# Sixty-four leftover rows of a contraction as row-tile pairs, and two weights side by side as one 512-column operand

## The chip, the cores and the metric

One core of one Trainium2 chip. The metric is the time of one execution in device microseconds, as the median of several runs.

## The reference

The model mixes two branches of an input x of 2048 x 576 with a learned gate, and returns the output and the gradients of everything:

```python
g   = sigmoid((x * gate_w).sum(-1))
a   = irfft2(rfft2(x) * (w_r + 1j * w_i))                 # global filter, 2-D FFT
b   = (gelu(x @ w_gate) * (x @ w_up)) @ w_down            # D=576 -> F=4608 -> D
out = g * a + (1 - g) * b
# and the vjp of out with grad_out: A_x, w_r, w_i, w_gate, w_up, w_down, gate_w
```

All in bf16. D = 576 = 4 x 128 + 64. Every product that contracts over D has four full chunks of 128 rows and one tail of 64.

## The kernel before

The loop that the change touches has 18 groups of 256 columns of F, with 8 steps each: 144 steps. A step takes 256 of the 2048 rows (two tiles of 128) and makes three products that contract over D: gate and up (x with w_gate, w_up) and dA (grad_out with w_down transposed). ScalarE takes them out of PSUM (the accumulator memory; the comments say how the pools divide its banks):

```python
ph = ps1.enter_context(tc.tile_pool(name="ph", bufs=4, space=PSUM))   # 1 bank each: products
pw = ps1.enter_context(tc.tile_pool(name="pw", bufs=2, space=PSUM))   # 1 bank each: weight gradients
pf = ps1.enter_context(tc.tile_pool(name="pf", bufs=1, space=PSUM))   # 2 banks, one buffer: FFT units

nc.gpsimd.memset(xT[0:D4NEW, 4, :, :], 0.0)      # 64 zero rows: the tail is padded to 128
...
def H_mm(g, tp):
    wg_g, wu_g, wdT_g = wts[g]
    out = []
    for w, xt in ((wg_g, xT), (wu_g, xT), (wdT_g, dOT)):
        pt = ph.tile([P, TPB, FG], F32, tag="hps", name="hps")         # FG = 256, TPB = 2
        for tt in range(TPB):
            for ci in range(5):
                nc.tensor.matmul(pt[:, tt, :], lhsT=xt[:, ci, tp * TPB + tt, :], rhs=w[:, ci, :],
                                 start=(ci == 0), stop=(ci == 4))
        out.append(pt)
    return out

def H_ew1(g, tp, pts):                            # VectorE's part of the chain cut
    hg, hu_ps, da_ps = pts
    ...
    nc.scalar.activation(q[:], hg[:], ACT.Square)
    nc.scalar.copy(xb[:], hg[:])
    ...
    nc.scalar.copy(hu[:], hu_ps[:])
    nc.scalar.activation(om[:], s[:], ACT.Sigmoid, scale=-2.0 * C_GELU)
    nc.scalar.activation(s[:], s[:], ACT.Sigmoid, scale=2.0 * C_GELU)
    ...                                           # for the two row tiles:
        nc.scalar.activation(da[:, tt, :], da_ps[:, tt, :], ACT.Copy, scale=omg32[:, t0 + tt:t0 + tt + 1])
```

The gap between the products of two steps is filled with FFT units (all through the one buffer `pf`) and with weight-gradient units of the group before:

```python
quota = [0, 1, 1, 1, 2, 1, 2, 1]                  # weight-gradient units by step of the group
for g in range(NG):
    for tp in range(NT):
        step = g * NT + tp
        fft_until(want(step, 0))                  # FFT unit(s) ahead of the products
        pts = H_mm(g, tp)
        tiles = H_ew1(g, tp, pts)                 # ScalarE: q, xb, hu, om, s, da
        fft_until(want(step, 1))                  # FFT unit(s) behind them
        H_ew2(g, tp, tiles)
        ...
        for _ in range(quota[tp]):
            if pend:
                pend.pop(0)()                     # weight-gradient units
```

Each FFT unit is some matmuls into `pf` and one copy out of it (its drain), mostly on ScalarE, so the drain stands in ScalarE's program behind the `da` of its step.

## Time and profile before

| | before |
|---|---|
| median of 4 runs (range) | 1579.05 us (1577.83 to 1579.81) |
| span of the profiled run | 1576.6 us |
| start: up to q of step 8 | 84.7 us |
| loop: q of step 8 to q of step 143 | 1016.2 us |
| rest | 475.7 us |

I cut the span at ScalarE's q of step 8 and of step 143. The table by stretches for these three parts of the kernel before: length, then busy time and instructions of TensorE, its weight loads, VectorE, ScalarE and GpSimd, then granted clock (the share of full speed that TensorE was given by the clock record), DMA share and GB/s.

```profile
0.00:84.70 84.70, 55.82 (x508) 44.98 (x509) 55.52 (x160) 58.33 (x101) 8.49 (x25) 0.90 0.64 165
84.70:1101.00 1016.30, 994.94 (x9043) 859.09 (x9041) 673.98 (x1816) 653.82 (x1251) 0.00 (x0) 1.00 0.42 117
1101.00:1576.60 475.60, 459.33 (x3764) 366.84 (x3761) 84.43 (x178) 26.63 (x45) 17.84 (x33) 0.99 0.85 171
```

TensorE works for 994.9 of the loop's 1016 us.

### The profile page before, as it was taken

The page shows a single profiled execution, that of the slowest core. Times are in us where ns is not written, and L with a number is a line of the kernel's source. Part 1 is how long each engine was busy: PE and PEld are TensorE (multiplying, and loading weights), DVE is VectorE, ACT ScalarE, POOL GpSimd, SP SyncE. Part 2 cuts the span into 40 slices and gives each one's busy share as a digit, 9 for nine tenths or more (in the row PEclk, how much of TensorE's full clock was granted, in tenths as well). Part 3 has the DMA queues.
Part 4 walks back from the last instruction along what each step waited for, and adds up shares of the span by engine and source line. Part 5 has one row for each costly group of instructions (what it writes and reads, how often), then busy time and mean ns, then how long its engine had stood idle before and what let it go on. Part 6 is the DMA issues. An engine that isn't in the chain of part 4 may idle for free.

```text
span 1576.6 us, 33157 instructions
## 1 busy us (share of the span) xinstructions
PE 1510.1 (96%) x13310; PEld 1270.9 (81%) x13310; DVE 813.9 (52%) x2154; ACT 738.8 (47%) x1395; POOL 26.3 (2%) x58
## 2 busy tenths in 40 slices
PE   6798999999999999999999999999997999999998
PEld 4577888888788888888888888888876777777776
DVE  5775565666887877865555646667103212121210
ACT  6777665765766766665666656656000000000000
POOL 1000000000000000000000000000000000000000
PEclk8999999999999999999999999999999999999999
DMA  6632432334544544453424434364899978787873
GB/s 140 198 102 78 113 99 82 109 97 132 140 134 120 151 124 129 132 152 93 124 82 135 127 97 128 101 145 122 241 192 214 212 153 172 155 171 154 170 150 69
DMA packets 513435, 214.45 MB, mean 136 GB/s; under 512 B 318080, under 2 KB 506368, under 8 KB 513280
## 3 DMA queue, kind: packets, MB, share of 16 engines
q1 hardware_dynamic: 511648, 207.61, 54.5%
q0 software_dynamic: 1632, 4.72, 1.1%
q8 instruction: 104, 1.70, 0.5%
q14 instruction: 51, 0.42, 0.1%
HBM read 41.77 MB, written 94.71 MB: 87 GB/s over the span
## 4 chain that ended last, share of the span: by engine, by line
PE 62%; issue 23%; DVE 6%; ACT 6%; DMA 1%; POOL 1%; SPq 1%; POOLq 0%; DVEq 0%; ACTq 0%
PE hps L312 25%; PE wps L392 15%; PE wps L376 7%; PE pf L640 3%; PE acc L833 2%; PE wps L403 2%; PE pf L433 2%; PE acc L875 2%; ACT da L334 1%; ACT om L330 1%; ACT q L323 1%; DMA pin<-scr 1%; PE pf L624 1%; PE pf L626 1%; ACT xb L324 1%
## 5 line engine op out<-in xcount | busy, mean ns | idle before, releaser
L312 PEld LDWEIGHTS <-xT 128*128 128x128 bf16 x2880 | 286.0, 99 | 39.6
L875 PEld LDWEIGHTS <-pin 128*128 128x128 bf16 x2304 | 225.4, 98 | 58.3 <-DMA pin<-scr 1.6
L392 PEld LDWEIGHTS <-xn 128*128 128x128 bf16 x2304 | 223.9, 98 | 30.3 <-issue 3.6
L312 PE MATMUL hps<-wg_g,xT 128*128 128x256 bf16 x1440 | 186.5, 278 | 0.0
L312 PE MATMUL hps<-wu_g,xT 128*128 128x256 bf16 x1440 | 183.8, 275 | 0.0
L312 PE MATMUL hps<-wdT_g,dOT 128*128 128x256 bf16 x1440 | 180.8, 273 | 0.0
L325 DVE TENSOR_SCALAR s<-q 128x512 bf16<-128x512 bf16 x144 | 42.0, 291 | 254.0 <-ACT q L323 253.8
L312 PEld LDWEIGHTS <-dOT 128*128 128x128 bf16 x1440 | 141.0, 98 | 16.4
L833 PE MATMUL acc<-wd_all,pin 128*128 128x288 bf16 x1152 | 145.4, 288 | 8.1 <-DMA pin<-scr 6.6
L376 PE MATMUL wps<-dB,A 128*128 128x288 bf16 x1152 | 152.2, 286 | 0.0
L875 PE MATMUL acc<-wuT,pin 128*128 128x288 bf16 x1152 | 143.4, 286 | 1.3 <-DMA pin<-scr 1.3
L833 PEld LDWEIGHTS <-pin 128*128 128x128 bf16 x1152 | 113.2, 98 | 38.5 <-DMA pin<-scr 7.5
L875 PE MATMUL acc<-wgT,pin 128*128 128x288 bf16 x1152 | 143.4, 286 | 0.0
L376 PEld LDWEIGHTS <-A 128*128 128x128 bf16 x1152 | 112.7, 98 | 27.6
L392 PE MATMUL wps<-dHu,xn 128*128 128x256 bf16 x1152 | 131.7, 273 | 0.0
L392 PE MATMUL wps<-dHg,xn 128*128 128x256 bf16 x1152 | 131.5, 273 | 0.0
L323 ACT ACTIVATE q<-hps 128x512 bf16<-128x512 f32 x144 | 86.1, 598 | 94.9 <-PE hps L312 94.9
L885 ACT COPY f32t<-acc 128x576 f32<-128x576 f32 x16 | 10.2, 638 | 250.5 <-PE acc L875 250.5
L334 ACT ACTIVATE da<-hps,omg 128x256 bf16<-128x256 f32 x288 | 118.1, 460 | 0.0
L887 DVE SCALAR_TENSOR_TENSOR f32t<-gwf,dlog,f32t 128x576 f32<-128x576 f32 x16 | 13.1, 818 | 179.1 <-ACT f32t L885 179.1
L330 ACT ACTIVATE om<-s 128x512 bf16<-128x512 bf16 x144 | 91.0, 632 | 24.5 <-DVE s L326 23.9
L331 ACT ACTIVATE s<-s 128x512 bf16<-128x512 bf16 x144 | 90.7, 630 | 4.6
(164 smaller groups left out, 1760.9 us busy)
## 6 DMA issues: line engine op xcount, KB each, us to landing
scr<-A SPq DMA_DIRECT2D x144, 128.0 KB, 1.9
scr<-dHg SPq DMA_DIRECT2D x144, 128.0 KB, 1.9
scr<-dHu SPq DMA_DIRECT2D x144, 128.0 KB, 1.9
out_dram<-dw SPq DMA_DIRECT2D x72, 128.0 KB, 1.8
out_dram<-dwd SPq DMA_DIRECT2D x36, 144.0 KB, 2.0
wd_all<-in_B_w_down_dram SPq DMA_DIRECT2D x3, 1728.0 KB, 12.6
scr_p<-Vt SPq DMA_DIRECT2D x32, 144.5 KB, 2.3
Vp<-scr_p SPq DMA_DIRECT2D x16, 289.0 KB, 3.4
```

Of the source, the lines that this page charges most:

```text
L312: nc.tensor.matmul(pt[:, tt, :], lhsT=xt[:, ci, tp * TPB + tt, :], rhs=w[:, ci, :], start=(ci == 0), stop=(ci == 4))
L323: nc.scalar.activation(q[:], hg[:], ACT.Square)
L325: V.tensor_scalar(s[:], q[:], A_GELU, 1.0, op0=ALU.mult, op1=ALU.add)
L330: nc.scalar.activation(om[:], s[:], ACT.Sigmoid, scale=-2.0 * C_GELU)
L331: nc.scalar.activation(s[:], s[:], ACT.Sigmoid, scale=2.0 * C_GELU)
L334: nc.scalar.activation(da[:, tt, :], da_ps[:, tt, :], ACT.Copy, scale=omg32[:, t0 + tt:t0 + tt + 1])
L376: nc.tensor.matmul(wps[:, :288], lhsT=tl(0, t)[:, fch * P:(fch + 1) * P], rhs=dB[:, t, h * 288:(h + 1) * 288], start=(t == 0), stop=(t == ...
L392: nc.tensor.matmul(wps[:, cc, :], lhsT=xn[:, t, (c0 + cc) * P:(c0 + cc + 1) * P], rhs=tl(k, t), start=(t == 0), stop=(t == T - 1))
L403: nc.tensor.matmul(wps[r0:r0 + 64, 0, :], lhsT=xn[:, t, 512:576], rhs=tl(k, t), start=(t == 0), stop=(t == T - 1))
L640: nc.tensor.matmul(yps[:, h, :288], lhsT=Z[:, lc, c, :], rhs=tb.At[lc][:, c, h * 288:(h + 1) * 288], start=(n == 0), stop=(n == 5))
L833: nc.tensor.matmul(bps[:, h, :288], lhsT=At[:, r, :], rhs=wd_all[:, fc, h * 288:(h + 1) * 288], start=(fc == 0), stop=(fc == NFC - 1))
L875: nc.tensor.matmul(xps[:, h, :288], lhsT=src[:, r, :], rhs=wT[:, h * 288:(h + 1) * 288], start=(k == 1 and f0 + r == 0), stop=(k == 2 and ...
```

## The change

The intent: the padded tail costs as much as a full chunk, though half its rows are zero. The change keeps a real 64-row tail in each half of the array's rows, and runs the tails of two row tiles at the same time, one per half. Gate and up stand side by side in one 512-column operand, so each weight load of x serves 512 columns. To keep the tails in few blocks, dA of two steps is computed at once, on even steps, ahead of gate and up. PSUM is re-cut for it: gate and up share one two-bank tile, dA of two steps another, one buffer each. The core of the diff (loads, transposes and index tables that follow from it are cut):

```diff
-    ph = ps1.enter_context(tc.tile_pool(name="ph", bufs=4, space=PSUM))
+    ph = ps1.enter_context(tc.tile_pool(name="ph", bufs=1, space=PSUM))
+    pz = ps1.enter_context(tc.tile_pool(name="pz", bufs=1, space=PSUM))
...
+LO, HI = slice(0, 64), slice(64, 128)
+    zt = [None]
     def H_mm(g, tp):
-        wg_g, wu_g, wdT_g = wts[g]
-        out = []
-        for w, xt in ((wg_g, xT), (wu_g, xT), (wdT_g, dOT)):
-            ...
-        return out
+        wgu, wdT = wts[g]
+        t0 = tp * TPB
+        if tp % 2 == 0:
+            zt[0] = pz.tile([P, 2, 2, FG], F32, tag="z", name="z")
+            for t in range(t0, t0 + 4):
+                for ci in range(4):
+                    nc.tensor.matmul(zt[0][:, t % 2, (t - t0) // 2, :], lhsT=dOT[:, ci, t, :], rhs=wdT[:, ci, :],
+                                     start=(t < t0 + 2 and ci == 0), stop=False)
+        xy = ph.tile([P, 2, 2 * FG], F32, tag="xy", name="xy")
+        for tt in range(TPB):
+            for ci in range(4):
+                nc.tensor.matmul(xy[:, tt, :], lhsT=xT[:, ci, t0 + tt, :], rhs=wgu[:, ci, :], start=(ci == 0), stop=False)
+        for tt, r in enumerate((LO, HI)):
+            nc.tensor.matmul(xy[:, tt, :], lhsT=xT[r, 4, t0 + tt, :], rhs=wgu[r, 4, :], start=False, stop=True)
+        if tp % 2 == 0:
+            for t in range(t0, t0 + 4):
+                r = (LO, HI)[t % 2]
+                nc.tensor.matmul(zt[0][:, t % 2, (t - t0) // 2, :], lhsT=dOT[r, 4, t, :], rhs=wdT[r, 4, :],
+                                 start=False, stop=t >= t0 + 2)
+        return xy[:, :, 0:FG], xy[:, :, FG:2 * FG], zt[0][:, :, tp % 2, :]
...                                               # FFT first stage
-                    for ci in range(5):
+                    for ci in range(4):
...
+                for c in range(2):
+                    r = (LO, HI)[c if src is xT else t % 2]
+                    nc.tensor.matmul(yps[:, c, :DF], lhsT=src[r, 4, t, :], rhs=tb.Dt[4][r, c, :], start=False, stop=True)
```

More of the change, by code (lines that the diff above doesn't have):

```diff
@@ L37 @@
 IMM = bass.MemoryType
-def load_w_dchunks(nc, eng, dst, w, fsl):
-    eng.dma_start(dst[:, 0:4, :], w[0:512, fsl].rearrange("(c p) f -> p c f", p=P))
-    eng.dma_start(dst[:, 4, :], w[DCH[4][0]:D, fsl])
+LO, HI = slice(0, 64), slice(64, 128)
 class Unit:
@@ L66, in iotas @@
     G.iota(tb.dcol[:, 0:4], pattern=[[128, 4]], base=0, channel_multiplier=1, **kw)
-    G.iota(tb.dcol[:, 4:5], pattern=[[0, 1]], base=DCH[4][0], channel_multiplier=1, **kw)
+    for r in (LO, HI):
+        G.iota(tb.dcol[r, 4:5], pattern=[[0, 1]], base=512, channel_multiplier=1, **kw)
     tb.krow = res.tile([P, P], F32, name="krow")
@@ L211, in load_w @@
         fsl = slice(g * FG, (g + 1) * FG)
-        wg_g = wpool.tile([P, 5, FG], BF16, tag="wg_g", name="wg_g")
-        wu_g = wpool.tile([P, 5, FG], BF16, tag="wu_g", name="wu_g")
-        wdT_g = wpool.tile([P, 5, FG], BF16, tag="wdT_g", name="wdT_g")
-        load_w_dchunks(nc, LD, wg_g, B_w_gate, fsl)
-        load_w_dchunks(nc, LD, wu_g, B_w_up, fsl)
-        LD.dma_start_transpose(wdT_g[:, 0:4, :], B_w_down[fsl, 0:512])
-        LD.dma_start_transpose(wdT_g[:, 4:5, :], B_w_down[fsl, DCH[4][0]:D])
-        return wg_g, wu_g, wdT_g
+        wgu = wpool.tile([P, 5, 2 * FG], BF16, tag="wgu", name="wgu")
+        wdT = wpool.tile([P, 5, FG], BF16, tag="wdT", name="wdT")
+        for k, w in enumerate((B_w_gate, B_w_up)):
+            cols = slice(k * FG, (k + 1) * FG)
+            LD.dma_start(wgu[:, 0:4, cols], w[0:512, fsl].rearrange("(c p) f -> p c f", p=P))
+            for r in (LO, HI):
+                LD.dma_start(wgu[r, 4, cols], w[512:D, fsl])
+        LD.dma_start_transpose(wdT[:, 4:5, :], B_w_down[fsl, DCH[4][0]:D])
+        LD.dma_start_transpose(wdT[:, 0:4, :], B_w_down[fsl, 0:512])
+        LD.dma_start(wdT[LO, 4, :], wdT[HI, 4, :])
+        return wgu, wdT
     def load_dOT(t):
@@ L223, in load_dOT @@
         LD.dma_start_transpose(dOT[:, 4:5, t, :], do_v[:, t, DCH[4][0]:D])
-    nc.gpsimd.memset(xT[0:D4NEW, 4, :, :], 0.0)
+    nc.gpsimd.memset(gwT[LO, 4:5], 0.0)
     ident = res.tile([P, P], BF16, name="ident")
@@ L230 @@
         nc.gpsimd.dma_start(gwT[:, 0:4], gate_w[0:512].rearrange("(c p) -> p c", p=P))
-        nc.gpsimd.dma_start(gwT[:, 4:5], gate_w[DCH[4][0]:D].rearrange("(p o) -> p o", o=1))
+        nc.gpsimd.dma_start(gwT[HI, 4:5], gate_w[512:D].rearrange("(p o) -> p o", o=1))
     def load_x(t0):
@@ L237, in load_do @@
         LD.dma_start(dB[:, t0:t0 + 4, :], do_v[:, t0:t0 + 4, :])
+    do_flat = grad_out[0].rearrange("(p t) d -> p (t d)", t=T)
     def load_dOT(t0):
@@ L241, in load_dOT @@
             LD.dma_start_transpose(dOT[:, 0:4, t, :], do_v[:, t, 0:512])
-            LD.dma_start_transpose(dOT[:, 4:5, t, :], do_v[:, t, DCH[4][0]:D])
-        nc.gpsimd.memset(dOT[0:D4NEW, 4, t0:t0 + 2, :], 0.0)
+            c0 = t * D + (512 if t % 2 == 0 else DCH[4][0])
+            LD.dma_start_transpose(dOT[:, 4:5, t, :], do_flat[:, c0:c0 + P])
     load_x(0)
@@ L269, in x_chunk @@
     def x_chunk(t0, act):
-        for k, c0 in enumerate((0, 2, 4)):
-            nc_ = min(2, 5 - c0)
-            tp_ = ph.tile([P, 2, 4, P], BF16, tag="hps", name="tp")
-            for c in range(nc_):
-                d0 = DCH[c0 + c][0]
-                for tt in range(4):
-                    nc.tensor.transpose(tp_[:, c, tt, :], xn[:, t0 + tt, d0:d0 + 128], ident[:])
-            p0 = D4NEW if c0 == 4 else 0
-            o, i = xT[p0:, c0:c0 + nc_, t0:t0 + 4, :], tp_[p0:, 0:nc_]
+        tp_ = ph.tile([P, 2, 2, 4, P], BF16, tag="xy", name="tp")
+        tl_ = pf.tile([P, 2, 2, 4, P], BF16, tag="pf", name="tl")
+        for h in range(2):
+            for c in range(2):
+                d0 = DCH[2 * h + c][0]
+                for tt in range(4):
+                    nc.tensor.transpose(tp_[:, h, c, tt, :], xn[:, t0 + tt, d0:d0 + 128], ident[:])
+        for tt in range(4):
+            for r in (LO, HI):
+                nc.tensor.transpose(tl_[r, 0, 0, tt, :], xn[:, t0 + tt, 512:D], ident[:])
+        for k in range(3):
+            o = xT[:, 2 * k:2 * k + 2, t0:t0 + 4, :] if k < 2 else xT[:, 4, t0:t0 + 4, :]
+            i = tp_[:, k] if k < 2 else tl_[:, 0, 0]
             if k in act:
@@ L303 @@
     kept = {}
+    zt = [None]
     def H_mm(g, tp):
-        wg_g, wu_g, wdT_g = wts[g]
-        out = []
-        for w, xt in ((wg_g, xT), (wu_g, xT), (wdT_g, dOT)):
-            pt = ph.tile([P, TPB, FG], F32, tag="hps", name="hps")
-            for tt in range(TPB):
-                for ci in range(5):
-                    nc.tensor.matmul(pt[:, tt, :], lhsT=xt[:, ci, tp * TPB + tt, :], rhs=w[:, ci, :],
-                                     start=(ci == 0), stop=(ci == 4))
-            out.append(pt)
-        return out
+        wgu, wdT = wts[g]
[18 more added lines that the diff above has]
+        return xy[:, :, 0:FG], xy[:, :, FG:2 * FG], zt[0][:, :, tp % 2, :]
     def H_ew1(g, tp, pts):
@@ L322, in H_ew1 @@
         xb, q, s, om, hu, da = (ewt(n) for n in ("xb", "q", "s", "om", "hu", "da"))
-        nc.scalar.activation(q[:], hg[:], ACT.Square)
-        nc.scalar.copy(xb[:], hg[:])
+        nc.scalar.activation(q[:], hg, ACT.Square)
+        nc.scalar.copy(xb[:], hg)
         V.tensor_scalar(s[:], q[:], A_GELU, 1.0, op0=ALU.mult, op1=ALU.add)
@@ L328, in H_ew1 @@
         V.tensor_tensor(q[:], xb[:], q[:], op=ALU.mult)
-        nc.scalar.copy(hu[:], hu_ps[:])
+        nc.scalar.copy(hu[:], hu_ps)
         nc.scalar.activation(om[:], s[:], ACT.Sigmoid, scale=-2.0 * C_GELU)
@@ L431, in f @@
                 for c in range(2):
-                    for ci in range(5):
+                    for ci in range(4):
                         nc.tensor.matmul(yps[:, c, :DF], lhsT=src[:, ci, t, :], rhs=tb.Dt[ci][:, c, :],
-                                         start=(ci == 0), stop=(ci == 4))
+                                         start=(ci == 0), stop=False)
+                for c in range(2):
+                    r = (LO, HI)[c if src is xT else t % 2]
+                    nc.tensor.matmul(yps[:, c, :DF], lhsT=src[r, 4, t, :], rhs=tb.Dt[4][r, c, :], start=False, stop=True)
                 ys[t] = unit([2, DF], name="Y")
@@ L463, in f @@
             for c in range(2):
-                for ci, (d0, dn) in enumerate(DCH):
-                    nc.tensor.transpose(tps[:, c, d0:d0 + dn], tb.Dt[ci][:, c, l0:l0 + ln], ident[:])
+                for ci in range(4):
+                    nc.tensor.transpose(tps[:, c, ci * P:(ci + 1) * P], tb.Dt[ci][:, c, l0:l0 + ln], ident[:])
+                nc.tensor.transpose(tps[:, c, 512:D], tb.Dt[4][LO, c, l0:l0 + ln], ident[LO, LO])
             o = unit([2, D], name="At")
```

## The prediction

> **What bounds the kernel now.** I read the busy shares first, then a table by stretches, then the timeline inside one step.
>
> ```profile
> PE 1510.1 (96%) x13310; PEld 1270.9 (81%) x13310; DVE 813.9 (52%) x2154; ACT 738.8 (47%) x1395; POOL 26.3 (2%) x58
> 86.00:1106.00 1020.00, 998.64 (x9077) 862.41 (x9076) 677.38 (x1826) 656.01 (x1255) 0.00 (x0) 1.00 0.42 117
> 1130.00:1577.00 447.00, 430.33 (x3492) 341.79 (x3489) 78.25 (x163) 21.00 (x33) 17.84 (x33) 0.99 0.84 168
> ```
>
> TensorE is busy for 98% of the stretch from 86 to 1106 us (the 144 steps of the gate/up/dA loop, less its start), VectorE and ScalarE for about 65%. The last 447 us (the second pass over the stored products) are not touched by the change and stay. So all that matters is the loop, and in it what TensorE does and waits for.
>
> One step with an FFT unit on either side of the gap (this is step 104, an even one; ScalarE and TensorE only):
>
> ```profile
> 812.05 1.26 PE L312 MATMUL hps<-wg_g,xT 128*128 128x256 bf16 x10
> 813.14 1.25 PE L312 MATMUL hps<-wu_g,xT 128*128 128x256 bf16 x10
> 813.34 0.60 ACT L323 ACTIVATE q<-hps 128x512 bf16<-128x512 f32 x1 [3.94 <-PE hps L312]
> 813.83 0.58 ACT L324 CAST xb<-hps 128x512 bf16<-128x512 f32 x1
> 814.23 1.26 PE L312 MATMUL hps<-wdT_g,dOT 128*128 128x256 bf16 x10
> 814.43 0.58 ACT L329 CAST hu<-hps 128x512 bf16<-128x512 f32 x1
> ...
> 816.11 0.82 ACT L334 ACTIVATE da<-hps,omg 128x256 bf16<-128x256 f32 x2
> 816.83 0.80 ACT L629 CAST ZT<-pf 128x768 bf16<-128x768 f32 x1
> 817.67 1.63 PE L640 MATMUL pf<-At,ZT 128*128 128x288 bf16 x12 [1.53 <-ACT ZT L629]
> 819.14 1.04 PE L312 MATMUL hps<-wg_g,xT 128*128 128x256 bf16 x8
> ```
>
> Four things are in it. Ten 256-column matmuls start every 1.09 us: 0.109 us each, a step's 30 take 3.27 us. ScalarE starts q 0.2 us after the gate product's last matmul interval, long before the step ends; hu follows to 1.57 us after q's start, da to 3.59 us after it, which is 1.61 us after the step's last matmul interval (815.32). The single FFT accumulator (pf) is drained in ScalarE's program order, after da. And the second FFT unit of a gap waits for that drain: 1.53 us here, the kind of wait the change can multiply.
>
> **What the Trainium skill says.** "TensorE: Matmul & The Clock Gate", Back-to-back issue gap, gives N/2.4 + 2.5 ns: 109 for 256 columns, as the trace has it, and 216 for 512, which no run here shows yet. "TensorEngine Tiling (Array Packing)", Key Properties: separate tiles work in parallel, and a change of tiling mode drains the engine. The trace agrees, on the column-tiled pairs of the weight-gradient tail:
>
> ```profile
> 733.37 0.27 PE L626 MATMUL pf<-Btab,Vp 128*128 128x256 bf16 x1
> 733.57 0.30 PE L403 MATMUL wps<-dHg,xn 128*64 128x256 bf16 x1
> 733.58 0.30 PE L403 MATMUL wps<-dHu,xn 128*64 128x256 bf16 x1
> ...
> 735.23 0.27 PE L403 MATMUL wps<-dHg,xn 128*64 128x256 bf16 x1
> 735.24 0.27 PE L403 MATMUL wps<-dHu,xn 128*64 128x256 bf16 x1
> 735.44 0.83 PE L392 MATMUL wps<-dHu,xn 128*128 128x256 bf16 x6
> ```
>
> A pair starts together and costs one interval (15 intervals in 1.66 us). Entering and leaving the mode takes 0.20 us from start to start, not 0.109: about 0.1 us per change. I assume the same for row tiles. "PSUM — Partial Sum Buffer", Specifications, has 8 banks of 512 fp32 columns: the pools of both kernels fill all 8. The tiling page's PSUM Bottleneck section warns that tiling speeds TensorE but not the evacuation. That is my main worry.
>
> **The change part by part.**
> *Matmul time, saved.* Two steps before: 60 x 0.109 = 6.54 us. After: 16 dA matmuls (1.74), 16 of 512 columns (3.45), two concurrent 512 pairs (0.43), two 256 pairs (0.22): 5.84 us. Saved 0.70 per two steps, 47 us over the 68 pairs after start-up.
> *Mode changes, added.* One into and one out of row mode per step: 136 x 2 x 0.1 = 27 us (entry 13.6, exit 13.5).
> *FFT first stage.* Its 5th chunk is a half-row pair; for x it saves one 0.12 us interval, for grad_out both halves are in the same row group and save nothing; two mode changes each. About 29 units remain after start-up: +4 us.
> *PSUM depth, lost.* Before, four 1-bank buffers rotate through three products, so a step never waits (none of the three product groups has idle time ahead of it). After, gate and up share one 2-bank tile with one buffer, dA another, with one buffer for two steps. So xy of step k+1 waits for hu of step k, and dA of the next even step for da of the odd step. And q can only start when both gate and up are complete: hu ends 1.76 us after an odd step's matmuls (0.2 + 1.56) and 1.56 after an even one's (dA tails come last there), da 3.75 and 3.55 after, where it was 1.61.
>
> To size it I took each of the 135 gaps between steps 8 and 143 with its own units from the timeline (units at 0.109 or 0.1225 us per matmul, a 32-matmul weight unit 3.49, a 16-matmul one 1.96), and let three rules act: the next xy or dA waits as above; a second FFT unit waits until ScalarE, after da, has drained the first (0.65 us, 0.80 for ZT); 0.06 us to release. With da at 1.61 these rules give 557 us of gaps; the trace has 573, and over steps 88 to 142 232.7 against 234.1, so they hold. With the new times:
> - xy/dA waits: 30 gaps, 29 us. By position in a group of eight: 8 us at 0 to 1 (no weight unit between, xy waits, e.g. 1.62 needed and 0.66 there), 9 at 1 to 2 and 11 at 3 to 4 (one 1.96 us unit, dA waits for 3.81).
> - pf waits: 44 gaps, +56 us. A gap of z, weight unit, d has its d start at 2.7 now; it will start at 3.55..3.75 + 0.80 + 0.06 = 4.4 to 4.6: +1.7 to 1.9.
> - gaps with two weight units (positions 4, 6) or a 3.49 one and little FFT (5, 7): near nothing.
>
> *Start-up.* Step 0 now needs four transposed rows of grad_out, not two, and dA comes first. The 4th lands about 20 us in the trace (its last transpose is issued at 16 us, 2.7 to land); the half-tile copy waits in the load queue for the weight transpose and two more loads go ahead: 3 to 4 us more. Step 0 ended at 14.3 us; some of that 8 to 10 us is swallowed by the wait for x that follows it now. I take +8.
>
> Sum: -47 + 27 + 4 + 29 + 56 + 8 = +77 us, so about 1656.
>
> **The rivals.**
> *Pure TensorE gain:* the stage is 98% TensorE, so fewer columns are time; -47 and no waits would give 1530. For it: zero idle before the product groups. Against: that zero idle was bought with four buffers, and pf already waits 1.5 us in this very trace.
> *Gain eaten by mode changes only:* if the new waits overlapped with each other or with TensorE work, -47 + 27 + 4 + 8 = -8, "same", 1571. For it: ScalarE has 35% to spare. Against: the waits are latency of one chain (q, xb, hu, om, s, da), which spare capacity does not shorten, and TensorE runs in program order.
> *Row pairs not concurrent:* then 0.65 us per two steps come back, +44 us more, near 1700. Against: column pairs run together in this trace.
> *VectorE becomes late:* its s chain feeds om; where steps come close together da was 3.0 us after the step instead of 1.61 (steps 129, 137). Shifting everything later could add some 5 to 10 us, or be swallowed where the gap is stretched anyway.
>
> **Range and chances.** Without any cost of a mode change my rules give 46 + 8, about 1633; with 0.15 us per change 81 + 8, 1668. Adding error in the waits (a third of 85 us either way) I take 1615 to 1700. Slower by over 2% (1611) fails only if most of the waits do not exist.
>
> **What would show it.** Right: the xy product group (512 columns) at about 0.216 us per matmul and the pairs starting together; idle before xy and dA groups released by ScalarE's hu and da, some 30 us; idle before the FFT units released by ScalarE's drains, rising by some 56 us; TensorE's busy share falling below 90% between 86 and 1106 us; the last stage unchanged at 447 us. Wrong: if pf waits stay near 20 us (then ScalarE's order is not as I read it), if mode changes show gaps well over or under 0.1 us, or if the loop's start slips by much more than 8 us.

## More of the kernel before

A difference between an experiment and the changed kernel crosses chips, on which the kernel before had medians of 1578 to 1582 us; read such differences as good to some 3 us.

The timeline of step 112 in the kernel before (start, length, engine, line, what; in brackets the idle time ahead of it and what ended it) has two FFT units in its gap, the case that will matter:

```profile
877.13 1.25 PE L312 MATMUL hps<-wg_g,xT 128*128 128x256 bf16 x10
...
878.42 0.60 ACT L323 ACTIVATE q<-hps 128x512 bf16<-128x512 f32 x1 [0.29 <-PE hps L312]
...
880.41 1.63 PE L640 MATMUL pf<-At,ZT 128*128 128x288 bf16 x12
...
881.20 0.82 ACT L334 ACTIVATE da<-hps,omg 128x256 bf16<-128x256 f32 x2
882.08 0.64 ACT L645 CAST yo<-pf 128x576 bf16<-128x576 f32 x1
882.77 0.27 PE L624 MATMUL pf<-Btab,Vp 128*128 128x256 bf16 x1 [0.73 <-ACT yo L645]
```

ScalarE starts q at 878.42, 1.99 us before the step's products end (880.41, where the first FFT unit begins). By the time TensorE needs the drain `yo` of that unit, ScalarE is nearly through, and TensorE loses 0.73 us.

## The result, and the profile after

| | before | after | difference |
|---|---|---|---|
| median of 4 runs | 1579.05 us | 1701.70 us | +122.7 |
| range | 1577.83 to 1579.81 | 1698.04 to 1707.02 | |
| start / loop / rest (profiled) | 84.7 / 1016.2 / 475.7 | 110.4 / 1111.6 / 478.8 | +25.7 / +95.4 / +3.1 |
| at half clock in start / loop | 17.1 / 3.4 us | 44.4 / 51.2 us | +27.3 / +47.8 |
| TensorE idle in the loop ahead of FFT units | 21.4 us | 71.0 us | +49.6 |
| ... ahead of the products | 0 | 37.6 us | +37.6 |

The ratio is 1.078, 95% interval 1.075 to 1.081: slower by over 2%. Ratios here and below are the mean time of one kernel's fast runs over that of the other's of the same rounds, so not quite the ratio of the medians quoted.

The first part of the page after, and the table by stretches after:

```profile
PE 1532.0 (90%) x11771; PEld 1091.4 (64%) x11886; DVE 812.7 (48%) x2154; ACT 730.0 (43%) x1395; POOL 22.5 (1%) x51
```
```profile
0.00:110.40 110.40, 69.97 (x456) 38.66 (x462) 54.85 (x160) 57.92 (x100) 4.62 (x18) 0.80 0.47 128
110.40:1222.00 1111.60, 1002.09 (x7576) 686.52 (x7682) 673.34 (x1816) 645.29 (x1250) 0.00 (x0) 0.98 0.38 108
1222.00:1700.90 478.90, 459.99 (x3744) 366.23 (x3744) 84.50 (x178) 26.74 (x45) 17.88 (x33) 0.99 0.85 169
```

Two things are odd at once. TensorE has 1467 fewer matmul records in the loop (some 115 of that are records missing from the trace) and yet is busy 7 us longer. And VectorE and ScalarE did the same work as before: nothing became busier, everything became later. The granted clock is down in the start (0.90 to 0.80) and in the loop (1.00 to 0.98).

Step 112 again, now in the kernel after (same columns; the step's gap holds the same two FFT units):

```profile
975.58 1.91 PE L323 MATMUL z<-wdT,dOT 128*128 128x256 bf16 x16
977.33 1.89 PE L328 MATMUL xy<-wgu,xT 128*128 128x512 bf16 x7
979.15 0.39 PE L330 MATMUL xy<-wgu,xT 64*128 64x512 bf16 x2
979.38 0.38 PE L334 MATMUL z<-wdT,dOT 64*128 64x256 bf16 x4
979.61 0.60 ACT L344 ACTIVATE q<-xy 128x512 bf16<-128x512 f32 x1 [3.03 <-PE xy L330]
979.69 1.64 PE L665 MATMUL pf<-At,ZT 128*128 128x288 bf16 x12
980.57 0.60 ACT L350 CAST hu<-xy 128x512 bf16<-128x512 f32 x1
982.37 0.82 ACT L355 ACTIVATE da<-z,omg 128x256 bf16<-128x256 f32 x2
983.08 0.64 ACT L670 CAST yo<-pf 128x576 bf16<-128x576 f32 x1
983.77 0.27 PE L649 MATMUL pf<-Btab,Vp 128*128 128x256 bf16 x1 [2.44 <-ACT yo L670]
```

The products do what they were meant to do. Sixteen dA matmuls take 1.75 us to the start of the next group, 0.109 each; the eight of 512 columns (one record is missing) take 1.82 us, which is eight times 0.216 and 0.1 for the change of mode; the two 512-column tails run together (0.23 us to the next pair), and the way out costs 0.1 again. A whole even step takes 4.11 us with both mode changes (975.58 to 979.69), which is what the prediction's terms add up to. But q starts at 979.61, only 0.08 us before the products end (979.69), where it had 1.99. So da and with it the drain `yo` come 1.9 us later relative to the products, and the wait of the second FFT unit grows from 0.73 to 2.44 us.

Where TensorE waits in the loop (waited for: us in all, times, longest us), first before, its costliest wait, then after:

```profile
PE pf L433 <- ACT Vt L452: 4.9, 5, 1.7
```
```profile
PE z L323 <- ACT da L355: 23.4, 16, 3.7
PE pf L454 <- ACT Vt L476: 14.8, 7, 3.5
PE pf L665 <- ACT ZT L654: 10.9, 7, 3.4
PE pf L608 <- ACT Vt L613: 10.6, 6, 3.4
PE pf L541 <- ACT Vt L613: 10.3, 3, 3.7
PE xy L328 <- ACT hu L350: 6.7, 7, 1.5
```

All of these are waits for ScalarE's place in a chain, while ScalarE itself is idle for over 40% of the loop. The rows `z` and `xy` are the single buffers; the rows `pf` are the FFT accumulator that was there before.

The start of the kernel after. Step 0 now begins with the dA of four row tiles and stops four times for transposed rows of grad_out:

```profile
12.47 1.03 PE L323 MATMUL z<-wdT,dOT 128*128 128x256 bf16 x4 [2.55 <-DMA dOT<-in_grad_out_dram]
14.93 1.03 PE L323 MATMUL z<-wdT,dOT 128*128 128x256 bf16 x4 [1.42 <-DMA dOT<-in_grad_out_dram]
19.32 1.03 PE L323 MATMUL z<-wdT,dOT 128*128 128x256 bf16 x4 [3.36 <-DMA dOT<-in_grad_out_dram]
...
24.35 0.60 ACT L344 ACTIVATE q<-xy 128x512 bf16<-128x512 f32 x1 [8.83 <-PE xy L330]
```

In the kernel before, step 0's gate product began at 9.51 us and step 0 was done at 14.3; here it is done at 24.4. The four matmuls above also show the half clock: 1.03 us against some 0.6 for four pipelined matmuls at 0.109.

And the half clock in the middle of the loop. Two dA groups of sixteen matmuls behind a wait, after:

```profile
1179.16 3.10 PE L323 MATMUL z<-wdT,dOT 128*128 128x256 bf16 x16 [2.46 <-ACT da L355]
1193.18 3.44 PE L323 MATMUL z<-wdT,dOT 128*128 128x256 bf16 x16 [1.99 <-ACT da L355]
```

The same group took 1.91 us in step 112. The clock record grants half speed for 3.4 us from 1179.7 and from 1193.4 on. So a wait costs twice: its own length, and slow matmuls behind it. I had not put that into the sum.

### The profile page after: what moved, and what is told of

Read it like the earlier page. It is cut to its first block, busy times and chain, and to the rows that moved or that the text cites. A ratio compares the mean times of both kernels' runs of the same rounds, so it can differ in the third digit from the quotient of the medians.

```text
span 1700.9 us, 30183 instructions
## 1 busy us (share of the span) xinstructions
PE 1532.0 (90%) x11771; PEld 1091.4 (64%) x11886; DVE 812.7 (48%) x2154; ACT 730.0 (43%) x1395; POOL 22.5 (1%) x51
## 4 chain that ended last, share of the span: by engine, by line
PE 65%; ACT 15%; issue 10%; DVE 6%; DMA 2%; SPq 1%; POOL 0%; DVEq 0%; POOLq 0%; ACTq 0%
PE xy L328 13%; PE wps L413 11%; PE acc L900 10%; PE z L323 8%; PE acc L858 7%; ACT da L355 3%; PE wps L397 3%; ACT q L344 3%; PE xy L330 3%; ACT om L351 2%; PE pf L665 2%; ACT xb L345 2%; PE wps L424 2%; ACT hu L350 1%; PE pf L454 1%
## 5 line engine op out<-in xcount | busy, mean ns | idle before, releaser
L328 PE MATMUL xy<-wgu,xT 128*128 128x512 bf16 x1037 | 273.5, 396 | 14.6 <-ACT hu L350 6.7
L344 ACT ACTIVATE q<-xy 128x512 bf16<-128x512 f32 x144 | 86.2, 598 | 344.9 <-PE xy L330 344.9
L328 PEld LDWEIGHTS <-xT 128*128 128x128 bf16 x1152 | 116.3, 102 | 127.2 <-issue 26.5
L323 PE MATMUL z<-wdT,dOT 128*128 128x256 bf16 x1152 | 153.7, 291 | 31.7 <-ACT da L355 23.4
L323 PEld LDWEIGHTS <-dOT 128*128 128x128 bf16 x1152 | 118.5, 104 | 59.5 <-issue 29.5
L355 ACT ACTIVATE da<-z,omg 128x256 bf16<-128x256 f32 x288 | 118.4, 461 | 0.0
L351 ACT ACTIVATE om<-s 128x512 bf16<-128x512 bf16 x144 | 90.7, 630 | 14.0 <-DVE s L347 13.5
L350 ACT CAST hu<-xy 128x512 bf16<-128x512 f32 x144 | 87.1, 605 | 0.0
```

The source lines that it names most:

```text
L323: nc.tensor.matmul(zt[0][:, t % 2, (t - t0) // 2, :], lhsT=dOT[:, ci, t, :], rhs=wdT[:, ci, :], start=(t < t0 + 2 and ci == 0), stop=False)
L328: nc.tensor.matmul(xy[:, tt, :], lhsT=xT[:, ci, t0 + tt, :], rhs=wgu[:, ci, :], start=(ci == 0), stop=False)
L344: nc.scalar.activation(q[:], hg, ACT.Square)
L350: nc.scalar.copy(hu[:], hu_ps)
```

## The experiments

Theory: the loss is lateness of ScalarE's chain. dA no longer runs behind gate and up, and the two products share a tile, so the chain starts when the step's products are over; FFT drains and the single buffers are waited for. Rivals: the mode changes and row tiles themselves; the reduced PSUM depth alone; the start-up alone. "Half clock" is the time at half speed in the clock record, the idle times are those ahead of the named groups; both for the loop.

| run | median us | ratio (95%) | start / loop | half clock | idle ahead of FFT / products |
|---|---|---|---|---|---|
| before | 1579.05 | | 84.7 / 1016.2 | 3.4 | 21.4 / 0 |
| after | 1701.70 | 1.078 (1.075 to 1.081) | 110.4 / 1111.6 | 51.2 | 71.0 / 37.6 |
| e1 no row tiles | 1707.27 | 1.082 (1.079 to 1.084) | 108.9 / 1123.7 | 47.8 | 70.7 / 37.3 |
| e2 dA last, each step | 1618.89 | 1.026 (1.024 to 1.027) | 88.8 / 1054.0 | 20.5 | 34.9 / 7.5 |
| e3 before, dA first | 1615.83 | 1.024 (1.022 to 1.025) | 91.3 / 1045.4 | 13.7 | 43.4 / 0 |
| e4 e2 in group 0 only | 1677.42 | 1.064 (1.061 to 1.066) | 88.9 / 1109.9 | 47.8 | 69.6 / 37.9 |
| e5 drain ahead of om, s, da | 1666.12 | 1.053 (1.052 to 1.055) | 109.4 / 1074.9 | 37.5 | 18.7 / 61.8 |
| e6 the same in before | 1581.71 | 1.000 (0.999 to 1.001) | 90.1 / 1010.7 | 5.2 | 13.9 / 0 |
| e7 before, gate and up in one tile | 1618.75 | 1.024 (1.022 to 1.026) | 90.8 / 1046.2 | 13.7 | 42.2 / 1.2 |
| e8 after, with filler matmuls | 1683.38 | 1.064 (1.063 to 1.066) | 112.0 / 1092.6 | 3.4 | 19.2 / 14.9 |
| e9 e3 and e7 together | 1682.85 | 1.064 (1.062 to 1.065) | 103.0 / 1097.2 | 44.4 | 77.9 / 1.2 |
| e10 e2 and e5 together | 1598.75 | 1.011 (1.009 to 1.012) | 93.2 / 1025.3 | 6.8 | 9.9 / 13.2 |
| e11 e6 from step 8 on | 1574.57 | 0.996 (0.994 to 0.997) | 84.5 / 1008.8 | 3.4 | 12.8 / 0 |

The kernel before had a median of 1578.07 beside e1 to e4, 1581.45 beside e5 to e8, and 1581.93 beside e9 to e11. All but e1 gave correct results.

### e1: the row tiles taken away

```diff
-lhsT=xT[r, 4, t0 + tt, :],  rhs=wgu[r, 4, :]
+lhsT=xT[:, 4, t0 + tt, :],  rhs=wgu[:, 4, :]        # likewise dA tails and the FFT's first stage
```

The result is wrong (the tail is counted twice, relative error 0.557).

> The changed kernel with every 64-row tail as an ordinary 128-row matmul (values wrong on purpose), so no row tiles and no mode changes in the loop; order and PSUM tiles as changed. Theory (late ScalarE chain and single buffers): gains 30 us of mode changes, loses the concurrent pairs, net about +16 us, 1718 us (1700 to 1730), the waits stay. Rival (mode changes and their drains are the cost): 1640 to 1680.

1707.27 us: without one mode change for row tiles the kernel is not faster (5.6 us slower by the medians, with ranges that overlap), and both waits are unchanged (70.7 and 37.3 us). The rival that mode changes cost the time falls. The run also prices the row tiles themselves: per two steps they save two 512-column and two 256-column intervals (0.65 us) and cost four changes of 0.1 us. The 0.25 us left make 17 us over 68 pairs of steps, less the 4 that the prediction charged to the pairs in the FFT's first stage. The loop of e1 is indeed 12.1 us longer, nearly all of it busy time (1014.8 against 1002.1 us); the medians differ by less because the start and the rest of e1 happen to be 1.5 and 2.9 us shorter.

### e2 and e4: dA behind gate and up

```diff
-        if tp % 2 == 0:                       # e4: only where g == 0
-            zt[0] = pz.tile(...); dA of four row tiles, ahead of xy
+        zt[0] = pz.tile(...)                  # every step
         xy = ...                              # unchanged, with its tails
+        for t in range(t0, t0 + 2): four dA matmuls
+        for t in range(t0, t0 + 2): the LO/HI tail pair
```

> The changed kernel with dA computed in each step, after gate and up, as row pairs; twice as many mode changes, xy and dA still single buffers. Theory (the order makes the ScalarE chain late): the chain starts 1.2 us before the end of the step's matmuls, pf and PSUM waits fall from about 97 to about 32 us over the loop, start-up nearly as before: 1610 to 1635 us. Rival (mode changes): 1702 plus 27, about 1730. Rival (single buffers whatever the order): 1690 to 1710.

> The changed kernel with dA per step and after gate and up in the first eight steps only. Theory (start-up waits for four rows of grad_out): step 8 starts 15 to 20 us earlier than at 105 us, and the time falls by as much, 1682 to 1690 us. Rival (the slip of the start is swallowed later): 1698 to 1704 us.

e2: 1618.89 us. It has twice the mode changes of the changed kernel, the same tiles and buffers in PSUM, and gives back 83 of the 123 us. What it changed is the order, with dA in every step instead of for two at once: products behind gate and up hide the first part of the chain again. e4 does it in the first of 18 groups alone and gives back 24.3 us, more than the 12 to 20 expected; its start is 88.9 us instead of 110.4 and its loop (1109.9) is that of the changed kernel. So dA for four row tiles at the start costs some 21.5 us, and the loop's share of the loss is elsewhere.

### e3: the order alone, in the kernel before

```diff
-        for w, xt in ((wg_g, xT), (wu_g, xT), (wdT_g, dOT)):
+        for w, xt in ((wdT_g, dOT), (wg_g, xT), (wu_g, xT)):
...
-        return out
+        return out[1:] + out[:1]
```

> The kernel before with one edit: dA is computed first in each step, gate and up after it; four buffers, no row tiles. Theory (late chain): da ends 2.7 us after the step's matmuls where it was 1.61, pf waits rise by about 25 us: 1595 to 1615 us. Rivals (single buffers, or mode changes): unchanged, 1579 within 4.

1615.83 us, just over the expected range and +38 beside its own runs of before, with four buffers, no row tile and not a matmul more. Its timeline in one step:

```profile
760.42 1.26 PE L312 MATMUL hps<-wg_g,xT 128*128 128x256 bf16 x10
761.51 1.26 PE L312 MATMUL hps<-wu_g,xT 128*128 128x256 bf16 x10
761.71 0.60 ACT L323 ACTIVATE q<-hps 128x512 bf16<-128x512 f32 x1 [4.10 <-PE hps L312]
...
762.60 0.27 PE L624 MATMUL pf<-Btab,Vp 128*128 128x256 bf16 x1
```

q starts 0.89 us before the products end (762.60) instead of 1.98: the chain is 1.09 us late, one product. The idle time ahead of FFT units doubles, from 21.4 to 43.4 us, with none ahead of the products. The lateness costs more than the waits it adds (22 us): TensorE's busy time in the loop rises by 7 us, beside 10 us more at half clock, and the start is 6.6 us longer.

### e5 and e6: the FFT drain moved up in ScalarE's order

```diff
         nc.scalar.copy(hu[:], hu_ps[:])
+        fft_until(want(step, 1))              # was after the whole of H_ew1
         nc.scalar.activation(om[:], s[:], ACT.Sigmoid, scale=-2.0 * C_GELU)
```

e5 has it in the changed kernel, e6 in the kernel before.

> The changed kernel with the FFT unit of the half step put ahead of ScalarE's two sigmoids and da, so that its accumulator is drained after hu instead of after da. Theory (one late chain, waited for in two places): the idle before FFT units falls from 71 to 15 to 25 us, but da is later by the drain, so the idle before dA and xy rises from 38 to 75 to 95 us: 1690 to 1698 us. Rival (the pf wait is a separate cost): idle before xy and dA stays at 38 us and the time falls by some 50 us, to 1650.

> The same move in the kernel before, where da gates nothing: the 21 us of idle before FFT units should fall by 4 to 12 us, 1567 to 1575 us; this would be faster than both kernels. Rival (ScalarE waits for the FFT unit and the sigmoids come late): 1579 or more.

e5: 1666.12 us. The idle time ahead of FFT units falls from 71.0 to 18.7 us, and the time by 36, less than the 52 taken away. The costliest waits in its loop, in the same columns as above:

```profile
PE z L323 <- ACT da L356: 46.3, 27, 4.0
PE pf L455 <- ACT Vt L477: 9.2, 4, 5.5
```

The wait of dA for da doubled, from 23.4 to 46.3 us: da now stands behind the drain, and moving work up in a FIFO moves the rest down. That trade was expected; my number for it was not. The time lies between what my theory gave (1690 and more) and what the rival gave (about 1650). I had charged da with the whole length of the drain; it seems that part of the drain lies in time in which ScalarE was waiting anyway. That reading is argued from the sizes and was not tested by itself.

e6: 1581.71 us, no gain where 1567 to 1575 was expected: the loop is 5.5 us shorter, the start 5.4 longer.

### e7: gate and up in one tile, in the kernel before

```diff
-    ph = ... bufs=4
+    ph = ... bufs=1                           # two banks, gate and up
+    pz = ... bufs=2                           # one bank each, dA
...
+        xy = ph.tile([P, 2, TPB, FG], F32, tag="hps", name="hps")
-            pt = ph.tile([P, TPB, FG], F32, tag="hps", name="hps")
+            pt = xy[:, len(out)] if len(out) < 2 else pz.tile([P, TPB, FG], F32, tag="z", name="z")
```

> The kernel before with gate and up in one two-bank tile with one buffer and dA in two one-bank buffers; order and matmuls unchanged. Theory (depth alone is cheap while dA comes last and hides the evacuation): only the gap after the first step of each group waits, 3 to 8 us in all: 1581 to 1587. Rival (single buffers are the cost): 1610 or more.

I meant it to price the lost PSUM depth and expected next to nothing. It took 1618.75 us, +37. The expectation was wrong, and not by way of the buffer: the idle time ahead of the products is 1.2 us. The timeline of one step:

```profile
758.96 1.26 PE L314 MATMUL z<-wdT_g,dOT 128*128 128x256 bf16 x10
759.16 0.60 ACT L325 ACTIVATE q<-hps 128x512 bf16<-128x512 f32 x1 [4.11 <-PE hps L314]
...
760.05 0.27 PE L626 MATMUL pf<-Btab,Vp 128*128 128x256 bf16 x1
```

q reads only the gate half of the tile, and yet starts 0.2 us after the up product is done, not after gate. The reader waits for the last write to the tile that it reads from. That is a lateness of 1.09 us again, reached in a different way than in e3, and the price in the loop is the same: 1046.2 against 1045.4 us long, 42.2 against 43.4 us of it idle ahead of the FFT units. The diff above leaves out that the edit also puts the start's transposes of x into dA's two buffers; there they wait 6.4 us for da, and the start is 6.1 us longer. So of the 37 us some 30 belong to the lateness.

### e9: both latenesses, in the kernel before

e3's and e7's edits together: the matmuls of the kernel before, with dA first and gate and up in one tile.

> The kernel before with both edits at once: dA first, and gate and up in one shared tile, so that the chain on ScalarE starts 2.1 us later in the step, as in the changed kernel; 256-column matmuls, no row tiles. Theory (time follows the lateness of the chain): 1.09 us late cost 37 us in two ways; 2.1 us late costs 67 by the gap rules plus some half-clock time, 1650 to 1675 us. Rival (the row tiles and the two-step dA tile make most of the changed kernel's loss): at most 1630.

1682.85 us, more than the 1650 to 1675 that I expected, and the strongest evidence: no row tile, no 512-column matmul, no new mode change, a matmul count equal to before, and over four fifths of the changed kernel's loss. How late it is shows in one step:

```profile
784.42 1.25 PE L314 MATMUL hps<-wu_g,xT 128*128 128x256 bf16 x10
785.51 2.12 PE L378 MATMUL wps<-dB,A 128*128 128x288 bf16 x16
785.71 0.60 ACT L325 ACTIVATE q<-hps 128x512 bf16<-128x512 f32 x1 [2.62 <-PE hps L314]
```

q starts 0.20 us behind the step's products (785.51), 2.18 us later than in the kernel before. That is slightly later than in the changed kernel's step 112 (1.91 us). By dose, for the loop: on time 1016 us, 1.09 us late 1045 and 1046, 2.18 us late 1097. The second microsecond costs more than the first. Of the changed kernel's 95.4 us in the loop e9 has 81.0; its start is 18.3 us longer than before, in part by e7's moved transposes. The stretch of its loop:

```profile
103.00:1200.20 1097.20, 1017.24 (x9042) 866.53 (x9041) 673.20 (x1816) 645.17 (x1250) 0.00 (x0) 0.98 0.39 109
```

The same matmuls as before are busy for 1017.2 instead of 994.9 us, beside 41 us more at half clock: about half of the time at half clock is lost.

### e8: filler matmuls in the changed kernel

```diff
             fft_until(want(step, 0))
+            if step in FILL:                  # 711 in 73 steps, where the trace had idle time
+                jk = pw.tile([P, 512], F32, tag="wps", name="jk")
+                for _ in range(FILL[step]):
+                    nc.tensor.matmul(jk[:, 0:FG], lhsT=xn[:, 0, 0:P], rhs=xn[:, 0, 0:FG], start=True, stop=True)
```

> The changed kernel with 711 filler matmuls (256 columns, never read, 78 us in all at full clock) put where the waits are, a little shorter than each wait. Theory (the idle itself costs more than its length, because it brings half-clock stretches): half-clock time in the loop falls from 51 us to under 15 and the time falls by 15 to 30 us, to 1672 to 1688, although work was added. Rival (half clock is a by-product without cost, or the fillers lengthen the path): 1700 or more.

1683.38 us: 711 useless matmuls, 711 x 0.109 = 77.5 us of TensorE work, make the kernel 18 us faster. The stretch of its loop:

```profile
112.00:1204.60 1092.60, 1057.57 (x8277) 747.97 (x8393) 672.99 (x1816) 644.93 (x1251) 0.00 (x0) 1.00 0.39 110
```

The clock is back at 1.00 (3.4 us at half speed, as before the change). Without the fillers the work is 1057.6 - 77.5 = 980.1 us. So the changed kernel's 1002.1 us hold some 22 us of half clock, and 980.1 - 994.9 = -14.8 is the change's own effect on the matmuls, for which the prediction has -47 + 27 + 4 = -16.

When does the clock drop? The drops lie on a fixed grid of 3.41 us. Laying that grid over the loops, I counted TensorE's idle time in each window. Idle time is what lies between TensorE's matmul records. In the changed kernel the 12 windows ahead of a drop have 1.99 to 3.29 us of idle time, the other 299 at most 2.03. In e9 the 8 have 2.02 to 2.95, the others at most 1.91; in e5 the 9 have 1.98 to 3.41, the others at most 1.98; in e3 the 4 have 2.41 to 2.63, the others at most 1.87. So some 2 us of idle time inside one window are enough (the line is not sharp: the one drop in e10's loop came behind 1.8 us). That is part of why the second microsecond of lateness costs more than the first. The first made the loop 29 us longer, the second 52; of the 23 us between them some 14 are more idle time and some 8 more busy time, as waits cross that line.

### e10: both edits in the changed kernel

e2's and e5's edits together, in the changed kernel.

> The changed kernel with dA per step and last, and with the early drain: both waits are taken away while row tiles, 512-column operand and single buffers stay. Theory: 8 to 15 us over before, 1587 to 1600 us. Rival (row tiles cost by themselves): not under 1610.

1598.75 us, within the expected 1587 to 1600. Row tiles, the 512-column operand and the single two-bank tiles are all still there; with 9.9 us ahead of FFT units and 13.2 ahead of products the kernel is 1.1% over before. The stretch of its loop:

```profile
93.20:1118.50 1025.30, 1001.98 (x7583) 674.58 (x7691) 672.07 (x1821) 643.19 (x1250) 0.00 (x0) 1.00 0.42 117
```

TensorE's 1002.0 us against 994.9 fit with why it cannot win: with dA in every step there are four mode changes a step, 136 x 4 x 0.1 = 54 us, against 47 us saved.

### e11: the early drain in the kernel before, without its loss at the start

```diff
+        if step >= 8:
+            fft_until(want(step, 1))          # between hu and om; below step 8 at its old place
```

> The kernel before with the early drain from step 8 on only, since in the run with it everywhere the loop was 5.5 us shorter and the start 5.4 us longer. Theory: 1572 to 1577 us, faster than both kernels by a small step. Rival: unchanged, 1579.

1574.57 us, ratio 0.9956 (0.9943 to 0.9969): faster than both kernels, by under half a per cent. The loop is 1008.8 us long instead of 1016.2, with TensorE's work unchanged at 994.7, and the start 84.5. The idle time ahead of FFT units fell from 21.4 to 12.8 us, and there is no single dA buffer to pay for it.

## Why the prediction was right or wrong, point by point

The direction and the mechanism were right; the size was too small (1656 for 1701.7, just above the range's end of 1700). Against the profiled difference of +124.3 us:

| term of the sum | predicted | measured | where |
|---|---|---|---|
| matmuls, mode changes, FFT first stage | -47 + 27 + 4 = -16 | -14.8 | e8's loop less its fillers |
| half clock in the loop | not in the sum | +22 | after against e8 |
| waits of xy and dA | +29 | +37.6 | loop, ahead of the products |
| waits of FFT units (pf) | +56 | +49.6 | loop, ahead of the FFT units |
| start-up | +8 | +25.7 | start; e4 takes 21.5 of it away |
| rest, and weight-gradient units | 0 | +3.1 and +1 | rest: 474 to 480 us in all runs, scatter |

The measured terms are readings of idle and busy time and good to a few us. Some 5 of the 37.6 us, and some 6 us of the -14.8, are not real: in most steps one record of the gate-up group is missing. Against that, idle time begins only where the record of the matmul ahead ends, some 0.16 us after the next one could have started, so each wait is read that much too short.

- **Bound and rules: right.** TensorE's program order and ScalarE's chain decide. Single waits came out to a few hundredths: where the gap holds too little work, the next xy was to start 1.62 us after an even step's last matmul interval, and does (1.62); the next dA 3.81 us after an odd step's, and 3.85 was measured. One reading was off: in the lines that the prediction shows, hu ends 1.67 us after q's start and not 1.57, because it waits there for the up product. The 1.56 that the sum uses is what the kernel after shows (980.57 + 0.60 against 979.61).
- **Mode changes of 0.1 us, pairs concurrent: right**, and by e1 not where the loss is. The rivals "row pairs not concurrent" and "eaten by mode changes only" fall.
- **"I take +8" for the start-up: failed.** The working saw step 0 end 8 to 10 us later (10 measured: 24.4 against 14.3), and hoped that some of it would be swallowed. Instead more was added: the waits for grad_out let the clock drop, with 44.4 us at half clock in the start instead of 17.1. The tables by stretches show what that cost: in the start TensorE is busy 14.2 us longer (55.8 to 70.0) with 52 fewer records, which fits half of the 27 us more being lost, and idle 11.5 us longer. Together they are the 25.7.
- **The missing term: failed.** The sum took 0.109 us for every 256-column matmul. The kernel before had next to no half clock in its loop, and I did not ask what the predicted idle time would do to the granted clock. My own list had 1.7 to 1.9 us coming on top of a pf wait like the 1.53 us shown; such gaps reached 2 us of idle time in a 3.41 us window in 12 places, for some 22 us.
- **"VectorE becomes late": not shown.** om waited 22.9 us for VectorE's s over the loop before the change and 13.5 after it, so the change did not make VectorE later on the whole. I found the gaps behind the second step of a group 12 us longer in all than the rules give, and a late s stands there (8.7 us of waits in those steps), but it stood there before as well (8.6), and the rules had left it out. No run tests this by itself.
- **The waits: about right in sum.** By these readings the xy and dA waits were underestimated by 9 us and the FFT waits overestimated by 6; the two errors nearly cancel, which is luck.
- **The checks named:** groups at 0.216, pairs together, waits for hu and da, drains waited for, the last stage unchanged: all as said. TensorE's busy share was to fall below 90% between 86 and 1106 us, and is 89.8% there (915.9 of 1020); it says little, as it is 90.1% over the loop and half clock counts as busy.
- **What the prediction did not separate:** it said that q can start only when both products are complete, and used it, but put the loss under "PSUM depth, lost". e3, e7 and e9 show that depth is the smaller part: e9, with next to no idle time ahead of the products (1.2 us), already has over four fifths of the loss, in the loop too.

What stays open: why e5's dA waits grew by less than the drain's full length would make them (argued above, not tested), and how the last 14 us of the loop's loss, which e9 does not have, divide among the waits for the single buffers and the new matmuls: no run separates them.

## What to carry to other kernels

When products are reordered or merged to feed TensorE better, ask first when their reader can start: the product that ran last was hiding the evacuation of the first ones, and a microsecond of lateness here cost 29 us over a loop of 135 steps, with no work added to any engine. Then ask what the new idle time does to the clock: on this core a wait that takes some 2 us out of a 3.41 us window is paid for again in slow matmuls, so a predicted sum of waits needs a term for it. And an engine with 40% to spare can still set the pace if its instructions stand in a chain.

## What the Trainium skill lacked or had wrong

- "TensorE: Matmul & The Clock Gate", "What's actually happening" and "Why this matters for your kernels": they have the clock fall back after an idle window of about 3.4 us, and warn of idle gaps over some 3 us (a later section says, without a figure, that frequent small idles can do it too). The free-running 3.41 us window agrees, but the drops came with far less: 1.99 to 3.29 us idle within the window (12 drops after the change; 299 other windows had at most 2.03). Filler matmuls that cut the idle time took half clock from 51.2 to 3.4 us and the time down by 18 us.
- "TensorE: Matmul & The Clock Gate", Back-to-back issue gap: it gives 216 ns for 512 columns as the isolated gap and about 131 ns sustained. Here eight sustained 512-column matmuls, each with its own weight load, took 0.216 us each; 0.131 was never seen. Its 0.109 for 256 columns agrees.
- "TensorEngine Tiling (Array Packing)", Key Properties: it says that a change of mode drains the engine, but not what that costs. It was 0.1 us each way, for row and column tiles, so one 64-row pair of 512 columns (0.216 us saved) pays for one entry and one exit and no more (with all its pairs, the changed kernel's loop is 12.1 us shorter than e1's, of 1112).
- "TensorEngine Tiling (Array Packing)", PSUM Bottleneck: the section warns of evacuation throughput alone. Here throughput was free (ScalarE 645 of 1112 us busy in the loop) and the evacuation's latency and order cost the time: 1683 us in e9, against 1582 beside it, with the matmuls of the kernel before.
- No page that I read says that a reader of one half of a PSUM tile may be held until the other half is written too. In e7, where each half fills a bank of its own, it delayed q by 1.09 us a step and made the loop 30 us longer.
